# Attention followed by an expert layer: moving one batch's last-column scores to another PSUM pair, and its product forward, in the steady down matmul

## The chip, the cores and the metric

One core of one Trainium2 chip. The metric is the device time of one execution in microseconds (us); a profile of one execution gives the trace that the argument reads. In the views PE is TensorE's matmuls and PEld its weight loads, ACT is ScalarE, DVE VectorE, POOL GpSimd; PSUM is the memory that TensorE writes its results to, in banks, and a pair is two of these. Lines such as L241 are lines of the kernel before; in the changed kernel the lines of the helpers that are named here are the same.

Most executions of a kernel agree within 0.3%. Some have a lower granted TensorE clock (0.981 to 0.989 on average instead of 0.997 to 1.000; one had 0.993) and are about 3 to 5 us longer, whatever the kernel. Where I name times of an experiment below, they are of executions with a clock of 0.997 or more, and I say how many there were.

## The reference, cut to what matters

```python
k_p = k.reshape(B, H, Sp, 8, D).mean(axis=3)        # B=8, H=8, S=576, Sp=72, D=64
v_p = v.reshape(B, H, Sp, 8, D).mean(axis=3)
attn = softmax(scale * q @ k_p^T)                   # per batch and head, 576 x 72
x = (attn @ v_p)  -> [4608 tokens, 512]
h = x @ w_in                                        # 512 -> 2048
out = (h * cos(h)) @ w_out                          # 2048 -> 512
```

A tile of the expert layer has 512 tokens, a batch has 576. So there are nine tiles for eight batches, and tile t + 1 needs the last 64 columns of batch t ("REST" in the kernel) as well as the first columns of batch t + 1.

## The kernel before

Each tile t has an up stage (64 matmuls of 512 columns, cosine on ACT, multiply on DVE) and a down stage (64 matmuls of 512 columns). The attention of the next batch is filled in between the down matmuls. A fill entry `(n, f)` runs `f` just ahead of the n-th down matmul; n is called its *place* here.

Attention is cut in units. Four big ones (256 columns x 4 heads) belong to batch b = t + 1, and REST (64 columns x 8 heads) to batch t. Each unit needs two things:

- *scores*: eight or four matmuls into a pair of PSUM banks, then one exponential on ACT that reads the pair;
- a *product* with the values: matmuls into a pair, then ln, ln, exp on ACT (the inverse of the sums), then two multiplies on DVE that read the pair and write `xT`.

```python
def scores(b, u, pair):
    scores_mm(b, u, pair)          # TensorE, L211
    scores_exp(b, u, pair)         # ACT: ex, L218

def values(b, u, pair, later=None):                 # the "product"
    ...                                             # matmuls, L241
    lnc, inv = inverse_tile(w)                      # lnc: one buffer
    for hp in range(2):
        nc.scalar.activation(out=lnc[half[1 - hp]], in_=pair[half[1 - hp], hp, 0:w], func=ACTF.Ln)   # L247
    nc.scalar.activation(out=inv, in_=lnc, func=ACTF.Exp, scale=-1.0)                                # L248
    def mul():
        for hp in range(2):
            nc.vector.tensor_mul(out=x_out(b, u, half[hp]), ...)                                     # L252
    ...
```

There are three pairs (`banks[0..2]`), which the up stage uses too, and two single banks for the down matmuls. The steady down stage (t = 1 to 6) before:

```python
fill = [(1, lambda: scores(t, REST, banks[1 if 0 < t and b < B else 2])), (12, lambda: values(t, REST, banks[1]))]
...  # (cut: t == 0)
elif b < B:
    fill = [(4, two_(0, 2, 0)), (14, V_(0, 1)), (19, V_(1, 2)),      # first two units: scores, products
            (31, two_(2, 0, 1)), (37, V_(2, 2)), (41, V_(3, 0)),     # last two units
            (42, fill[0][1]), (54, fill[1][1])]                      # REST: scores, product
...
for n, (ms, fc) in enumerate(mms):
    while fi < len(fill) and fill[fi][0] <= n:
        fill[fi][1]()
        fi += 1
    down_mm(obanks[ms % 2], ms, fc)
    if fc == FFCH - 1:
        down_out(t, ms, obanks[ms % 2])     # DVE copy L316, then the output DMA
```

`two_(n, p, q)` makes the scores of units n and n + 1 in pairs p and q; `V_(n, p)` is the product of unit n in pair p.

The softmax here doesn't subtract the row's maximum and nothing guards it: scores larger than these inputs give would overflow.

## Time and profile before

| | before |
|---|---|
| time, median (range, runs) | 305.17 us (304.85 to 305.43, 4) |
| span in the profile | 303.0 us |
| TensorE busy | 292.3 us, 96% |
| one steady down stage, from ACT's table load to the first up matmul | 16.48 us, six times the same |
| TensorE standing still in each | 0.31 us |

With TensorE at 96%, the question is where it still stands, not how busy the others are on average. The prediction below shows the lines and reads them. (It was made with the first three runs, whose median is 305.36.)

### The profile page before, as it was taken

Reading aid. Unit: us, or ns where it says so; the run is one execution under the profiler, and the core shown is the slowest. Engines: PE = TensorE matmul, PEld = TensorE weight load, DVE = VectorE, ACT = ScalarE, POOL = GpSimd, SP = SyncE. Lnnn points to the kernel's source line nnn. Section 1 sums busy time; section 2 is a strip of 40 time slices with the busy share of each in tenths; the row PEclk is TensorE's granted clock in tenths of the full one; section 3 lists DMA queues with packets and bytes.
Section 4 is the critical chain, followed back from the end, with each engine's and each line's share of the span. In section 5 each row is a group of like instructions: output and inputs, shape, how many; then the busy total and the mean of one; then the engine's idle time right before and its main releaser. Section 6 shows DMA issues by size and latency. Waiting matters only on the chain.

```text
span 303.0 us, 4567 instructions
## 1 busy us (share of the span) xinstructions
PE 292.3 (96%) x1766; PEld 141.8 (47%) x1798; DVE 172.8 (57%) x211; ACT 206.8 (68%) x255; POOL 129.8 (43%) x92
## 2 busy tenths in 40 slices
PE   6899999999999999999999999999999999999995
PEld 2545544444544444444444544454444544444444
DVE  6458646564656465736575566656574657425712
ACT  3887896469866986698668876788569856605500
POOL 8553008975963893369534972399000000000000
PEclk9999999999999999999999999999999999999999
DMA  7999999739476935693369426952800330031032
GB/s 144 203 207 206 208 204 195 161 55 172 94 167 88 151 70 129 101 163 82 80 117 165 96 65 126 162 107 54 151 0 2 70 69 0 22 84 35 0 71 71
DMA packets 44006, 32.92 MB, mean 109 GB/s; under 512 B 22096, under 2 KB 39248, under 8 KB 43984
## 3 DMA queue, kind: packets, MB, share of 16 engines
q0 software_dynamic: 19744, 18.07, 38.4%
q1 hardware_dynamic: 24080, 14.42, 20.8%
q8 instruction: 14, 0.23, 0.3%
q10 hardware_dynamic: 160, 0.13, 0.2%
q14 instruction: 8, 0.07, 0.1%
HBM read 36.70 MB, written 9.44 MB: 152 GB/s over the span
## 4 chain that ended last, share of the span: by engine, by line
PE 88%; ACT 5%; issue 2%; DMA 2%; DVE 1%; DVEq 0%; ACTq 0%; POOLq 0%
PE bank L297 41%; PE obank L310 35%; PE bank L241 5%; PE bank L211 3%; DMA q_b<-in_q_dram 2%; ACT lnc L247 2%; ACT ex L218 1%; PE bank L328 1%; DVE xT L252 1%; ACT inv L248 1%; PE obank L157 0%; ACT L285 0%; PE obank L192 0%; ACT cos L304 0%; PE bank L165 0%
## 5 line engine op out<-in xcount | busy, mean ns | idle before, releaser
L310 PE MATMUL obank<-w_out_sb,g_sb 128*128 128x512 bf16 x542 | 130.5, 380 | 0.9
L297 PE MATMUL bank<-xT,w_in_sb 128*128 128x512 bf16 x563 | 125.7, 379 | 1.3
L304 ACT ACTIVATE cos<-bank,half_pi 128x1024 f32<-128x1024 f32 x72 | 80.0, 1113 | 62.2 <-PE bank L297 62.2
L307 DVE TENSOR_TENSOR g_sb<-bank,cos 128x1024 bf16<-128x1024 f32 x72 | 88.1, 1225 | 51.7 <-ACT cos L304 51.7
L297 PEld LDWEIGHTS <-w_in_sb 128*128 128x128 bf16 x576 | 56.1, 98 | 69.0 <-issue 2.8
L310 PEld LDWEIGHTS <-g_sb 128*128 128x128 bf16 x560 | 52.3, 98 | 57.0 <-issue 3.1
L252 DVE TENSOR_TENSOR xT<-bank,inv 64x512 bf16<-64x512 f32 (+1 forms) x72 | 45.3, 629 | 46.7 <-ACT inv L248 45.2
L141 POOL TENSOR_TENSOR kv_st<-kv_st 72x2048 f32<-72x2048 bf16 x12 | 48.7, 4062 | 35.0 <-DMA kv_st<-in_k_dram 35.0
L247 ACT ACTIVATE lnc<-bank 64x512 f32<-64x512 f32 (+1 forms) x72 | 39.2, 544 | 6.6 <-PE bank L241 5.6
L218 ACT ACTIVATE ex<-bank 72x1024 bf16<-72x1024 f32 (+1 forms) x40 | 35.5, 926 | 3.3 <-PE bank L211 3.2
L316 DVE COPY o_sb<-obank 128x512 f32<-128x512 f32 x35 | 24.2, 692 | 17.0 <-PE obank L310 13.4
L142 POOL TENSOR_TENSOR kv_st<-kv_st 72x1024 f32<-72x1024 f32 x12 | 28.2, 2348 | 1.0
L248 ACT ACTIVATE inv<-lnc 128x512 f32<-128x512 f32 (+1 forms) x36 | 21.0, 583 | 1.1
L241 PE MATMUL bank<-ex,vz 72*128 72x256 bf16 (+1 forms) x176 | 20.0, 243 | 0.2 <-ACT ex L218 0.2
L241 PEld LDWEIGHTS <-vz 72*128 72x128 bf16 x176 | 13.6, 97 | 10.2 <-DVE xT L252 1.7
L145 POOL TENSOR_TENSOR kp<-kv_st 72x512 bf16<-72x512 f32 x12 | 15.0, 1268 | 0.5
L211 PE MATMUL bank<-qT,kk 64*72 64x256 bf16 (+1 forms) x192 | 13.6, 252 | 0.9 <-ACT qT L193 0.5
L211 PEld LDWEIGHTS <-kk 64*72 64x72 bf16 x192 | 7.5, 109 | 11.1 <-issue 9.8
L285 ACT ACT_TABLE_LOAD x9 | 11.5, 1283 | 0.9 <-PEq L514 0.7
L288 ACT ACT_TABLE_LOAD x9 | 11.5, 1283 | 0.2
L494 POOL COPY gate<-kk 1x1 bf16<-1x1 bf16 x5 | 0.9, 179 | 24.1 <-DMA kk<-kp 24.1
L84 POOL DMA_DIRECT2D q_b<-in_q_dram x10 | 7.7, 772 | 2.8 <-DMA w_in_sb<-in_moe_w_in_dram 1.4
(55 smaller groups left out, 88.2 us busy)
## 6 DMA issues: line engine op xcount, KB each, us to landing
out_dram<-o_sb SPq DMA_DIRECT2D x70, 128.0 KB, 2.3
kv_st<-in_v_dram POOLq DMA_DIRECT2D x8, 576.0 KB, 13.3
kv_st<-in_k_dram POOLq DMA_DIRECT2D x7, 576.0 KB, 7.9
q_b<-in_q_dram POOLq DMA_DIRECT2D x6, 576.0 KB, 10.2
w_in_sb<-in_moe_w_in_dram POOLq DMA_DIRECT2D x4, 512.0 KB, 13.3
w_out_sb<-in_moe_w_out_dram POOLq DMA_DIRECT2D x4, 512.0 KB, 18.4
q_b<-in_q_dram POOLq DMA_DIRECT2D x4, 288.0 KB, 11.9
g_sb<-in_k_dram SPq DMA_DIRECT2D x1, 576.0 KB, 3.6
```

The costliest lines, as they stand in the source:

```text
L141: add(out=s, in0=x[:, :, 0:4, :], in1=x[:, :, 4:8, :], op=ADD)
L142: add(out=s[:, :, 0:2, :], in0=s[:, :, 0:2, :], in1=s[:, :, 2:4, :], op=ADD)
L211: nc.tensor.matmul(pair[:Sp, bank, c:c + n].rearrange("p (g n) -> p g n", n=64), lhsT=kk[b % 2][half[r], h0 + i, 0:Sp], rhs=att["qT", b][h ...
L218: nc.scalar.activation(out=ex[:, 0:nh * n].rearrange("p (a n) -> p a n", a=2), in_=pair[:Sp, :, 0:nh * n // 2], func=ACTF.Exp, scale=scale ...
L241: nc.tensor.matmul(pair[:, hp, (i // 2) * n:(i // 2 + 1) * n], lhsT=vz[b % 2][:, pj, 2 * hp:2 * hp + 2, :].rearrange("p a d -> p (a d)"), ...
L247: nc.scalar.activation(out=lnc[half[1 - hp]], in_=pair[half[1 - hp], hp, 0:w], func=ACTF.Ln)
L252: nc.vector.tensor_mul(out=x_out(b, u, half[hp]), in0=cols(pair[half[hp], hp, :], u), in1=cols(inv[half[1 - hp]], u))
L297: nc.tensor.matmul(h[:, j, :], lhsT=w_in_sb[fc // 4][:, ki, (fc % 4) * 128:(fc % 4 + 1) * 128], rhs=xT[:, ki, t * TILE:(t + 1) * TILE], st ...
L304: nc.scalar.activation(out=cos, in_=h, func=ACTF.Sin, bias=half_pi[:, :1])
L307: nc.vector.tensor_mul(out=g_sb[:, 2 * fp:2 * fp + 2, :], in0=h, in1=cos)
L310: nc.tensor.matmul(o, lhsT=g_sb[:, fc, ms * 128:(ms + 1) * 128], rhs=w_out_sb[fc // 4][:, fc % 4, :], start=(fc == 0), stop=(fc == FFCH - 1))
L316: nc.vector.tensor_copy(out=o[:, 0:n], in_=ps)
```

## The change

The intent is to let REST's exponential run early, so that its product can stand further from the end of the stage, and the next up stage need not wait for it. The pair that the second product has left (pair 2) takes REST's scores; the third and fourth products move to pairs 0 and 1.

```diff
-            fill = [(1, lambda: scores(t, REST, banks[1 if 0 < t and b < B else 2])), (12, lambda: values(t, REST, banks[1]))]
+            late = 0 < t and b < B
+            fill = [(1, lambda: scores(t, REST, banks[2])), (12, lambda: values(t, REST, banks[2 if late else 1]))]
...
-            fill = [(4, two_(0, 2, 0)), (14, V_(0, 1)), (19, V_(1, 2)), (31, two_(2, 0, 1)), (37, V_(2, 2)),
-                    (41, V_(3, 0)), (42, fill[0][1]), (54, fill[1][1])]
+            fill = [(4, two_(0, 2, 0)), (14, V_(0, 1)), (19, V_(1, 2)), (32, two_(2, 0, 1)), (36, fill[0][1]),
+                    (38, V_(2, 0)), (41, V_(3, 1)), (45, fill[1][1])]
```

## The prediction

> **What bounds the kernel now.** I read the page first: the busy row and the chain of work that ended last.
>
> ```profile
> PE 292.3 (96%) x1766; PEld 141.8 (47%) x1798; DVE 172.8 (57%) x211; ACT 206.8 (68%) x255; POOL 129.8 (43%) x92
> ...
> PE 88%; ACT 5%; issue 2%; DMA 2%; DVE 1%; DVEq 0%; ACTq 0%; POOLq 0%
> ```
>
> TensorE sets the time: 96% busy and 88% of the chain. A change that neither adds nor removes matmuls can therefore only win back the moments in which TensorE stands still. The 5% of ACT and 1% of DVE in the chain say where to look for those, and also cap what there is to win. The changed code is the steady down stage (t = 1 to 6), so next I cut the trace by that stage, from the load of the exponential's table to the first matmul of the next up stage.
>
> ```profile
> 68.25:84.73 16.48, 16.28 (x104) 8.07 (x101) 9.67 (x15) 14.96 (x22) 13.31 (x6) 1.00 0.69 121
> 99.88:116.36 16.48, 16.28 (x105) 8.06 (x102) 9.68 (x15) 14.97 (x22) 16.16 (x7) 1.00 0.49 88
> ...
> 226.37:242.85 16.48, 16.28 (x104) 8.05 (x101) 9.67 (x15) 14.97 (x22) 0.00 (x0) 1.00 0.14 33
> ```
>
> Columns: stretch, its length, busy time of PE, PEld, DVE, ACT, POOL, granted clock, DMA share, GB/s. All six stages last 16.48 us to the hundredth, at full clock, whatever the DMA and GpSimd do, so one stage can be worked out and multiplied by six. I take t = 2. Its part of the chain of waits, in order of time:
>
> ```profile
> 112.79 1.03 PE obank L310 x4
> 113.82 0.30 PE bank L241 x8
> ...
> 114.20 0.38 ACT lnc L247
> 114.59 0.39 ACT lnc L247
> 115.00 0.43 ACT inv L248
> ...
> 115.88 0.44 DVE xT L252
> 116.36 5.99 PE bank L297 x27
> ```
>
> The last product of the stage (the eight 64-column matmuls of the batch before, REST) goes through logarithm, exponential and multiply before the next up matmul may start at 116.36. Now the timeline of the same stretch (start, length, engine, line, operation):
>
> ```profile
> 107.16 1.39 DVE L252 TENSOR_TENSOR xT<-bank,inv 64x512 bf16<-64x512 f32 x2
> ...
> 108.60 0.46 PEld L241 LDWEIGHTS <-vz 72*128 72x128 bf16 x4 [0.19 <-DVE xT L252]
> ...
> 109.43 1.19 ACT L247 ACTIVATE lnc<-bank 64x512 f32<-64x512 f32 x2 [0.17 <-PE bank L241]
> ...
> 111.32 1.19 ACT L247 ACTIVATE lnc<-bank 64x512 f32<-64x512 f32 x2
> ...
> 113.08 0.57 ACT L218 ACTIVATE ex<-bank 72x512 bf16<-72x512 f32 x1
> 113.21 1.39 DVE L252 TENSOR_TENSOR xT<-bank,inv 64x512 bf16<-64x512 f32 x2 [0.50 <-ACT inv L248]
> ...
> 113.94 2.32 PE L310 MATMUL obank<-w_out_sb,g_sb 128*128 128x512 bf16 x10
> 114.20 0.77 ACT L247 ACTIVATE lnc<-bank 64x256 f32<-64x256 f32 x2 [0.54 <-PE bank L241]
> ...
> 116.36 6.85 PE L297 MATMUL bank<-xT,w_in_sb 128*128 128x512 bf16 x30
> ```
>
> The ten down matmuls from 113.94 take 2.32 us with the last one's 0.38, so they start every (2.32 - 0.38)/9 = 0.216 us. The last starts at 115.88; the next could start at 116.10 and starts at 116.36: TensorE stands still for 0.26. It stands still once more, for about 0.05, where REST's product waits for its exponential (113.08 + 0.57 = 113.65; first product matmul at 113.71, 0.27 after its predecessor in the single records instead of 0.22). So there is 0.31 us to win per stage, 6 x 0.31 = 1.9 us in all, 0.6% of 305.36. That is the ceiling.
>
> **What the Trainium skill says.** "TensorE: Matmul & The Clock Gate", section "Wait — 56ns, not 53.3ns?", gives N/2.4 GHz plus about 2.5 ns between starts of warm matmuls, 215.7 ns at 512 columns; this trace has 0.216, so TensorE has no slack besides the two stops. "ScalarE: Activation LUTs", section "What ACT_TABLE_LOAD costs", gives 186 ns plus 0.833 ns per element for an activation with immediate scale, and an overlap of 93 ns back to back. The trace has 1.02 for 1024 columns (formula 1.04), 0.59 for 512 (0.61), 0.38 for 256 (0.40). Two score exponentials start 0.92 apart, with the overlap, but the ln, ln, exp group of one product does not overlap like that: its next group starts 1.89 later (109.43 to 111.32), as each step reads what the last one wrote and there is one lnc buffer. "Perfetto Trace Analysis", section "Matmuls", advises to rotate independent groups through different PSUM banks, so that emptying one overlaps the next group's matmuls. The weight load at 108.60 shows what the present layout lacks: the third product reuses pair 2 and is released by the multiplies of the second (107.16 + 1.39 = 108.55); its matmul still starts on the beat, at 108.74.
>
> **The change part by part.** Counts and shapes stay the same on every engine; the instruction order of both programs confirms it (PE has 3598 rows in each). Four things move.
>
> 1. Second score group from place 31 to 32: one down matmul goes ahead, +0.216. Scores start at 107.10 instead of 106.88, the first exponential at 107.55 instead of 107.33. The pairs are free; no stop.
> 2. REST's scores from place 42 to 36, into pair 2. After the score group (0.56) and four down matmuls, and the 0.31 that separates a down matmul from scores after it in this trace, they are due at 107.10 + 0.56 + 0.65 + 0.01 + 0.31 = 108.63. Pair 2 must have been left by the second product's multiplies: end 108.55, release some 0.05 later, 108.60. It fits with 0.03 to spare. These matmuls move, they are not added: 0.25 earlier in the stage and 0.25 less later.
> 3. Third product at 38 in pair 0, fourth at 41 in pair 1. The third is due at 108.63 + 0.25 + 0.23 + 0.22 = 109.33, against 108.74: 0.59 later (0.25 REST's scores, two places, a little rounding). REST's exponential now lies between the scores' exponentials and this product's logarithm: 107.55 + 2 x 0.92 = 109.39 to 109.96, before the logarithm can start (109.43 + 0.59 = 110.02). So it costs ACT nothing.
> 4. REST's product at 45 instead of 54: nine matmuls, 1.9 us, earlier on TensorE. But this doesn't reach the end whole, since ACT isn't ready for it. ACT: third product from 110.02, fourth from 111.91, REST from 113.80 (1.89 each), its last exponential ends 1.22 later (114.20 to 115.42 before), at 115.02. Before: 115.42. DVE: the fourth product's multiplies start when its inverse ends, 113.21 + 0.59 = 113.80, and last 1.39, to 115.20; REST's two follow (DVE copies the third output block after them now, no longer between) and last 0.87: 116.07. Before: 115.44 + 0.87 = 116.31.
>
> The next up matmul follows 0.05 after the last multiply, at about 116.12, against 116.36: 0.24 us per stage. TensorE would be there at 116.36 - 0.31 = 116.05, so a stop of some 0.07 remains. One item more: in the changed order the wait for these multiplies sits on the weight load ahead of the first up matmul, not on the matmul, so the load can't be done early. A load held in the same way at the start of the kernel (copy of qT ends 8.50, load 8.55, matmul 8.56) lost only 0.01 between load and matmul, so I charge 0.02: 0.22 us. Sum: 6 x 0.22 = 1.3 us; 305.36 - 1.3 = 304.0 (the span of the profile 303.0 to 301.7).
>
> **The rivals.** First, the stop vanishes wholly: nine places earlier looks like 1.9 us of slack against a stop of 0.26, and the time falls by the ceiling, to 303.5. What speaks against it is the ACT row: once the third product is late, ACT and then DVE work through to the end without a pause. Second, the wait for pair 2 takes the place of the one removed. Only 0.03 spare it; every hundredth by which REST's scores slip delays the third product and the whole ACT and DVE chain behind it. A slip of 0.1 leaves 0.12 a stage, 304.6. For it: the release is from exactly those multiplies; against it: the held load at 108.60 cost nothing before. Third, the held weight load costs its full 0.10 at the up stage: 0.14 a stage, 304.5. Fourth, the later output copies or the DMA matter: the copy of block two moves from 114.63 to about 116.1, but its accumulator is wanted only at the next down stage, some 14 us on, and the first multiply of the up stage comes at 119.43. No effect.
>
> **Range and chances.** Mechanisms give 0.12 to 0.31 a stage, 0.7 to 1.9 us; the mean is near 1.3. The runs of before spread over 0.46, so a median carries some 0.2. Time 304.0, range 303.3 to 304.8. Two per cent is 6.1 us, three times the ceiling: faster 0.01, same 0.98, slower 0.01 (an unforeseen stop of over 1 us in each stage).
>
> **What would show it.** In the timeline of t = 2: REST's scores on the beat after four down matmuls, the third product's logarithm about 0.6 later than before, REST's logarithm directly after the fourth product's inverse with no idle time, and DVE's four last multiplies back to back. The stage should last 16.48 - 0.22 = 16.26. If it lasts 16.17, the stop vanished, and my ACT and DVE chain is too long; if over 16.35, the wait for pair 2 or the weight load binds. The prediction is wrong if stages t = 1 to 6 no longer agree with each other or if time moves outside them.

## The result, and the profile after

| | before | changed |
|---|---|---|
| time, median (range, runs) | 305.17 (304.85 to 305.43, 4) | 303.81 (303.58 to 303.91, 4) |
| ratio of the fast runs (95% interval) | | 0.9955 (0.9938 to 0.9972) |
| steady down stage | 16.48 | 16.26 |
| from the table load of t = 1 to that of t = 7 | 189.74 | 188.47 |

A ratio is the mean time of one kernel's fast runs over that of the other's fast runs of the same rounds, so it isn't quite the ratio of the medians. The gain is 1.36 us, 0.45%: clear of noise, and inside two per cent, as forecast. The table loads of t = 1 and t = 7 enclose the six steady ends of stage; between them 1.27 us went, six times 0.21.

The stretches of the changed kernel, in the same columns as in the prediction:

```profile
...
100.06:116.31 16.25, 16.25 (x106) 7.96 (x101) 8.98 (x14) 15.15 (x22) 14.84 (x6) 1.00 0.57 102
...
```

The stage has lost 0.22 us, and all six agree (16.25 or 16.26). DVE has one instruction less in it (14 instead of 15): the copy of the third output block, 0.69 us, has gone behind REST's multiplies, and starts only 0.03 before the first up matmul. Both traces record 1798 weight loads, 211 DVE and 255 ACT instructions in all: only the order has changed. Now the timeline of t = 2 after the change (start, length, engine, line, operation, what ended the idle time):

```profile
107.33 1.39 DVE L252 TENSOR_TENSOR xT<-bank,inv 64x512 bf16<-64x512 f32 x2
...
107.72 2.41 ACT L218 ACTIVATE ex<-bank 72x1024 bf16<-72x1024 f32 x3 [0.68 <-PE bank L211]
...
108.80 0.21 PEld L211 LDWEIGHTS <-kk 64*72 64x72 bf16 x8 [0.42 <-DVE xT L252]
...
110.20 1.20 ACT L247 ACTIVATE lnc<-bank 64x512 f32<-64x512 f32 x2
...
112.13 4.27 PE L310 MATMUL obank<-w_out_sb,g_sb 128*128 128x512 bf16 x19
...
113.98 0.77 ACT L247 ACTIVATE lnc<-bank 64x256 f32<-64x256 f32 x2
113.98 2.28 DVE L252 TENSOR_TENSOR xT<-bank,inv 64x512 bf16<-64x512 f32 x4 [0.50 <-ACT inv L248]
...
114.77 0.42 ACT L248 ACTIVATE inv<-lnc 128x256 f32<-128x256 f32 x1
...
116.28 1.29 DVE L316 COPY o_sb<-obank 128x512 f32<-128x512 f32 x2
116.31 0.76 PEld L297 LDWEIGHTS <-w_in_sb 128*128 128x128 bf16 x5 [0.41 <-DVE xT L252]
116.31 1.04 PE L297 MATMUL bank<-xT,w_in_sb 128*128 128x512 bf16 x4
```

Read it from the end. The first up matmul at 116.31 follows the last of DVE's four multiplies, which end at 113.98 + 2.28 = 116.26. The nineteen down matmuls from 112.13 start (4.27 - 0.38)/18 = 0.216 apart, the last at 116.02; the next could start at 116.24 and starts at 116.31. So a stop of 0.08 us is left of 0.26. The other stop, 0.05 ahead of REST's product, is gone: in the single records that product starts at 111.89, 0.21 after the down matmul ahead of it. DVE's four multiplies stand as one group, since the copy is no longer between them; they start when the fourth product's inverse is ready. REST's logarithm at 113.98 has no idle time before it, where it had 0.54 before: ACT now goes through all three products without a pause from 110.20 on. REST's inverse ends at 114.77 + 0.42 = 115.19, while DVE is busy with the fourth product's two multiplies until 115.37; so at the end DVE binds, and ACT has 0.18 to spare. The three exponentials from 107.72 include REST's.

Here a view misleads. The chain of waits of the same stage:

```profile
112.29 4.10 PE obank L310 x19
116.39 6.78 PE bank L297 x31
```

ACT and DVE have vanished from it, as though TensorE ran through. They haven't: the wait now sits on the weight load, not on the matmul, and the modelled length of a matmul (0.38 for a beat of 0.216) covers a stop of 0.08. The starts of the matmuls show the stop; the chain does not. Nor is the view of waits a measure of it:

```profile
PEld L297 <- DVE xT L252: 2.5, 6, 0.4
```

That is 2.5 us of weight loads held in six stages, while TensorE itself lost 6 x 0.08 = 0.5 us.

### The profile page after: what moved, and what is told of

It reads as the page before. It is cut to its first block, busy times and chain, and to the rows that moved or that the text cites. A ratio compares the mean times of both kernels' runs of the same rounds, so it can differ in the third digit from the quotient of the medians.

```text
span 302.1 us, 4605 instructions
## 1 busy us (share of the span) xinstructions
PE 294.0 (97%) x1798; PEld 141.6 (47%) x1798; DVE 172.3 (57%) x211; ACT 206.8 (68%) x255; POOL 129.8 (43%) x92
## 4 chain that ended last, share of the span: by engine, by line
PE 85%; DMA 10%; POOL 2%; ACT 1%; issue 0%; DVE 0%; POOLq 0%; ACTq 0%
PE obank L310 39%; PE bank L297 37%; DMA w_out_sb<-in_moe_w_out_dram 6%; PE bank L241 5%; DMA w_in_sb<-in_moe_w_in_dram 4%; PE bank L211 3%; PE bank L328 1%; POOL kv_st L84 1%; POOL kp L384 1%; POOL q_b L84 1%; ACT L285 0%; ACT cos L304 0%; ACT ex L218 0%; POOL identity masks.py:197 0%; DVE o_sb L316 0%
## 5 line engine op out<-in xcount | busy, mean ns | idle before, releaser
L310 PE MATMUL obank<-w_out_sb,g_sb 128*128 128x512 bf16 x560 | 132.5, 380 | 0.5 <-DMA w_out_sb<-in_moe_w_out_dram 0.5
```

Of the source, the lines that this page charges most:

```text
L310: nc.tensor.matmul(o, lhsT=g_sb[:, fc, ms * 128:(ms + 1) * 128], rhs=w_out_sb[fc // 4][:, fc % 4, :], start=(fc == 0), stop=(fc == FFCH - 1))
```

## The experiments

The theory is that of the prediction: in the steady stage, ACT works without a pause through the third and the fourth product (ln, ln, exp, twice), and DVE then through the four multiplies of the fourth and REST's product, so the *third product's place* sets when the next up stage may start, until TensorE's own work sets it. REST's product has slack, provided that its exponential comes early and that its multiplies stand ahead of DVE's third copy. The chief rival is the simple reading of the change: REST's product is nine places earlier, and each place is worth something. All runs below were correct. The stage length is that of t = 2, and the other five agree with it within 0.01 us. The runs lay on several chips (the first four below the changed kernel on one, the last four on another), on which the kernel before took 304.90 and 305.20 at a clock of 0.997 or more; so the comparison rests on the stages, and the times are its check.

| run | places: group, REST's scores, third, fourth, REST's product | stage, expected | stage, measured | time (executions at clock 0.997 or more) |
|---|---|---|---|---|
| changed | 32, 36, 38, 41, 45 | 16.26 | 16.26 | 303.81 (4) |
| product_47 | 32, 36, 38, 41, **47** | 16.26 | 16.26 | 304.03 (4) |
| product_48 | 32, 36, 38, 41, **48** | 16.95 | 16.98 | 308.08 (3) |
| group_31 | **31**, 36, 38, 41, 45 | 16.26 | 16.26 | 303.94 and 303.98 (2) |
| rest_scores_35 | 32, **35**, 38, 41, 45 | 16.45 | 16.46 | 304.92 (3) |
| third_40 | 32, 36, **40**, **43**, 47 | 16.69 | 16.69 | 306.32 and 306.78 (2) |
| third_37 | **31**, 36, **37**, **40**, 45 | 16.17 | 16.18 | 303.05 (5) |
| scores_only | 32, 36, 38, 41, **54** | 16.95 | 16.98 | 308.01 and 308.32 (2) |
| product_only_47 | before, with REST's product at **47** | 17.7 | 17.74 | 312.51 (3) |

### product_47 and product_48: how much slack has REST's product?

```diff
-                    (38, V_(2, 0)), (41, V_(3, 1)), (45, fill[1][1])]
+                    (38, V_(2, 0)), (41, V_(3, 1)), (47, fill[1][1])]     # product_48: 48
```

> The changed kernel with REST's product at place 47 instead of 45, still ahead of the copy of the third output block. Chain theory (ACT and DVE from the third product on set the end; REST's product has slack): the steady stage stays at 16.26 us, time as the changed kernel, 303.8. Place theory (each place that REST's product is earlier wins time): 0.43 us per stage lost, 16.69, until the whole gain is gone, 305.2 or more.

> One place further, 48, so that DVE's copy of the third output block is issued ahead of REST's multiplies. Chain theory with DVE's order: DVE is busy with the fourth product until about 15.3 us into the stage, the copy takes 0.7, so REST's multiplies end at about 16.9 and the stage lasts 16.95 (0.69 more than changed, 0.47 more than before): 6 x 0.69 = 4.1 us, 307.9. If the order on DVE does not matter and only ACT's chain does: 16.26, 303.8.

Two places later changed nothing: 16.26. One more place cost 0.72 us per stage, 4 us in the whole. The place differs by a single beat of 0.216 between the two, and TensorE's work not at all. What differs is that the third output block ends at place 47, so that from 48 on its copy is issued to DVE ahead of REST's multiplies. DVE in product_48, end of t = 2:

```profile
119.18 1.39 DVE L252 TENSOR_TENSOR xT<-bank,inv 64x512 bf16<-64x512 f32 x2 [0.50 <-ACT inv L248]
...
120.60 0.69 DVE L316 COPY o_sb<-obank 128x512 f32<-128x512 f32 x1
...
121.32 0.86 DVE L252 TENSOR_TENSOR xT<-bank,inv 64x256 bf16<-64x256 f32 x2
```

REST's inverse was ready at 120.39, so its multiplies could have started when the fourth product's ended, at 120.57; the copy holds them up until 121.32. The place theory falls with the first run, and the importance of DVE's order is shown by the pair. (The profile of product_48 fell in an execution with a low clock early on. Its steady stages ran at full clock, and the run scores_only below, at full clock throughout, shows the same 16.98.)

### group_31: is the shift of the second score group worth anything?

```diff
-(32, two_(2, 0, 1)), (36, fill[0][1]),
+(31, two_(2, 0, 1)), (36, fill[0][1]),
```

> The changed kernel with the second score group back at place 31. Chain theory: the third product keeps its place 38, and it alone starts the chain, so the shift by one is worth nothing: stage 16.26, 303.8. If the shift was part of the gain (scores later, fewer stops elsewhere): over 16.26, up to 16.48.

The stage stayed at 16.26 in all six. This part of the change is idle. Two of four executions, the profiled one among them, had a clock of 0.989 and 0.983 and took 307.0 and 307.2; in the profiled one the low clock lies in the first tenth of the span, ahead of the steady stages. Therefore the median of all four (305.50) is not used.

### rest_scores_35: the wait for pair 2

```diff
-(32, two_(2, 0, 1)), (36, fill[0][1]),
+(32, two_(2, 0, 1)), (35, fill[0][1]),
```

> REST's scores one place earlier, at 35. My step 2: the second product's multiplies leave pair 2 about 8.66 us into the stage, release at 8.72, and at place 36 the scores are due at 8.75; at 35 they are due at 8.53 and must wait 0.19. The chain behind slips by that: stage 16.45, six times 0.19 = 1.15 us, 304.9. If pair 2 is free much earlier than I worked out: 16.26, 303.8.

The timeline of t = 2 in this run:

```profile
107.40 1.39 DVE L252 TENSOR_TENSOR xT<-bank,inv 64x512 bf16<-64x512 f32 x2
...
108.84 0.21 PEld L211 LDWEIGHTS <-kk 64*72 64x72 bf16 x8 [0.63 <-DVE xT L252]
```

The second product's multiplies end at 107.40 + 1.39 = 108.79, and REST's scores start at 108.84, 0.05 later, although they were one place earlier. The stage grew by 0.20. So the wait for pair 2 is real, and the change just clears it, though one place earlier would not: REST's scores at 36 start 8.75 us into the stage, where the pair is free from about 8.72.

### third_40 and third_37: where does the chain start?

```diff
# third_40
-                    (38, V_(2, 0)), (41, V_(3, 1)), (45, fill[1][1])]
+                    (40, V_(2, 0)), (43, V_(3, 1)), (47, fill[1][1])]
# third_37
-(32, two_(2, 0, 1)), (36, fill[0][1]), (38, V_(2, 0)), (41, V_(3, 1)), (45, fill[1][1])]
+(31, two_(2, 0, 1)), (36, fill[0][1]), (37, V_(2, 0)), (40, V_(3, 1)), (45, fill[1][1])]
```

> Third product at 40 instead of 38, fourth at 43, REST's product at 47 (shown or not shown to be free by the run with 47 alone). Chain theory: the ACT and DVE work behind the third product starts 2 x 0.216 = 0.43 us later and so does the next up stage: 16.69, 6 x 0.43 = 2.6 us, 306.4. Rival (the chain starts elsewhere, for instance at the fourth product or at REST's exponential): no change, 16.26.

> Second score group at 31, third product at 37, fourth at 40, the rest as changed. Chain theory: the chain starts 0.216 us earlier than in the changed kernel, which is more than the 0.08 us of stop that the changed kernel still has; the stop goes, TensorE alone sets the stage: 16.17, 6 x 0.08 = 0.5 us less, 303.3. Rival (the remaining stop is the cost of a weight load that is held and can't be done early): 16.26 stays, 303.8.

Two places later gave 16.69, two beats of 0.216 more; since place 47 for REST's product cost nothing above, the delay comes from the third and fourth products. One place earlier gave 16.18. This is the run group_31 with these two products one place forward, so the 0.08 belongs to them. The end of t = 2 in third_37:

```profile
111.79 4.27 PE L310 MATMUL obank<-w_out_sb,g_sb 128*128 128x512 bf16 x19
...
113.42 2.28 DVE L252 TENSOR_TENSOR xT<-bank,inv 64x512 bf16<-64x512 f32 x4 [0.50 <-ACT inv L248]
...
115.89 1.46 PE L297 MATMUL bank<-xT,w_in_sb 128*128 128x512 bf16 x6
```

The multiplies end at 115.70. The last down matmul starts at 111.79 + 18 x 0.216 = 115.68, and the up matmul at 115.89, on the beat. The stop is gone. The first up matmul's weight load still waits for the multiplies here, but is released at 115.75, 0.14 ahead of its matmul, and so this run alone doesn't show what a load costs that is held to the last moment. The changed kernel does: there load and matmul start within 0.01 of each other, and the second up matmul follows 0.226 after the first (116.310 to 116.536 in the single records), where it is 0.216 here and 0.215 in the kernel before. In all eight traces in which load and matmul start together it is 0.225 to 0.227, in the other four 0.215 or 0.216. So a load held to the last moment costs 0.01, not 0.08, and the rival, that it was the rest of the stop, falls.

Which of the two products starts the chain was not tried apart, but the traces tell. In the changed kernel the fourth product's matmuls end by 111.19 as recorded and its logarithm starts at 112.09, straight after the third product's exponential; the fourth was there some 0.8 us before ACT was. The third product's matmuls end at 110.10, and its logarithm follows at 110.20. In group_31 ACT even stands idle for 0.27 until the third product comes, with the same stage. So it is the third.

This version is faster than the kernel before, by a ratio of 0.9931 (0.9918 to 0.9944): 303.05 (302.95 to 303.24, five runs). It never ran in the same rounds as the changed kernel; that it is faster than that one too is shown by the stages, 16.18 against 16.26.

### scores_only and product_only_47: each part of the change alone

```diff
# scores_only: from the changed kernel
-(45, fill[1][1])]
+(54, fill[1][1])]
# product_only_47: from the kernel before
-(41, V_(3, 0)), (42, fill[0][1]), (54, fill[1][1])]
+(41, V_(3, 0)), (42, fill[0][1]), (47, fill[1][1])]
```

> One part alone: REST's scores at 36 in pair 2 and the products moved as in the change, but REST's product left at place 54. Chain theory: ACT starts REST's logarithm at 14.3 us into the stage as before, but DVE is busy with the fourth product until 15.3 and then with the copy until 16.0; REST's multiplies end at 16.9, stage 16.95, slower than both kernels: 307.9. Place theory: the product has its old place, so the time is that of before, 305.2.

> The other part alone: the kernel before with only REST's product moved from 54 to 47, scores left at 42 in pair 1. REST's exponential still stands behind the fourth product on ACT and ends 13.8 us into the stage, so TensorE, due at 12.3, waits until 13.83 and has 17 down matmuls left: stage 17.7, 1.24 more than before, 6 x 1.24 = 7.4 us, 312.6. Rival (the place of the product is the gain, the scores' place doesn't matter): 16.2 to 16.3, about 304.

In scores_only the end of t = 2 looks as in product_48: DVE's multiplies of the fourth product from 114.77 to 116.16, the copy from 116.19 to 116.88, REST's multiplies from 116.92 to 117.78, and the first up matmul at 117.83. The copy stands between the fourth product's multiplies and REST's, and the up matmul waits for it all. The scores' move without that of REST's product is a loss of 0.50 us per stage against the kernel before. (It brings the later third product and the new pairs with it.) The product's move alone is a larger one:

```profile
114.84 0.57 ACT L218 ACTIVATE ex<-bank 72x512 bf16<-72x512 f32 x1
115.47 0.39 PE L241 MATMUL bank<-ex,vz 72*128 72x64 bf16 x8 [1.40 <-ACT ex L218]
```

REST's exponential is still behind the fourth product on ACT and ends at 115.41; TensorE waits for it and the stage lasts 17.74. So neither part gains anything alone, at the places tried; the gain needs both.

### A last stop outside the change, and the changed kernel again

```diff
# third_37_last_14: third_37, and
-(12, lambda: values(t, REST, banks[2 if late else 1]))
+(14, lambda: values(t, REST, banks[2 if late else 1]))
```

> The version with the third product at 37, and in the last down stage with a product (t = 7, not steady, not part of the change) REST's product at place 14 instead of 12: in the changed kernel TensorE stands there for 0.32 us, waiting for REST's exponential; two down matmuls (0.43) cover it. Expected 0.3 us less than with the third product at 37 alone, near 302.8, and the steady stages stay at 16.18. If another wait sets the end of that stage: as the version before it, 303.1.

> The changed kernel once more, on the same chip as the best version, so that the two are compared in the same rounds: 303.8, stages of 16.26.

The changed kernel gave 303.72 (six executions), its stages 16.25 to 16.26. The new version gave 303.14 (five executions at full clock, 302.76 to 303.83; a sixth took 307.69). In the traces, the part from the table load of t = 7 to the end went from 44.96 in third_37 to 44.65, 0.31 less, as expected. In the times this isn't seen: 303.14 on this chip against 303.05 for third_37 on another. In its profiled execution the table load of t = 1 came at 68.77, in third_37's at 68.39, and this start of the kernel, which no edit here touches, varied by that much. So the 0.31 is shown by the trace alone.

## Why the prediction was right

It was right in its mechanism as well as in its number: each step of its sum can be set beside the trace. Where two small errors cancelled, this is said.

- *The ceiling of 0.31 us per stage.* third_37 reached 16.18, 0.30 below the kernel before, with TensorE on its beat at the end.
- *The second score group one place later.* Predicted as no stop and no gain; group_31 shows it idle.
- *REST's scores at 36 clear the wait for pair 2 by 0.03.* They start 8.75 us into the stage, as worked out, and one place earlier the wait appeared, 0.20 long for 0.19 expected.
- *The third product 0.59 later.* Its logarithm starts 10.14 us into the stage instead of 9.56: 0.58. The prediction's sum of times was right, but not the split given in brackets (0.25 for REST's scores and two places make 0.68): the product moved by one place, 0.22, and REST's scores hold up the down matmuls by 0.36, with the changes into and out of them (109.28 for a start due at 108.92).
- *ACT's and DVE's chain up to 16.19 us into the stage (116.07 in the times of the kernel before).* The last multiply ends at 16.20. The four multiplies together take 2.28 instead of the 2.26 that two groups of 1.39 and 0.87 add up to. The reason given for the 1.89 of a product on ACT, that each step reads what the last one wrote, isn't shown: the second logarithm reads nothing of the first, and yet starts 0.60 after it, at a length of 0.59. The 1.89 itself came from the trace. (The page's 186 ns are for an immediate scale and an immediate bias; the quotation leaves out the bias, and the durations fit.)
- *The charge of 0.02 for the held weight load.* The wait did move to the load, as predicted, but the term was oversized, and in the wrong place: the matmul started 0.05 after the last multiply both before (116.31 to 116.36) and after (116.26 to 116.31). The load's cost is the 0.01 ahead of the second up matmul, outside the stage as cut here. That the multiplies took 0.02 longer and the sum stayed 0.22 is luck, on a scale of 0.02.
- *Six times 0.22, 1.3 us, 304.0.* Measured: 0.22 per stage, 1.36 in the medians, 303.81. From one table load to the next it is 0.21, as the held load takes 0.01 back.

The first rival, that the stop vanishes wholly, was wrong for this kernel, and for the stated reason: the third product had been moved back. third_37, which moves it forward again, is what that rival described. The second rival was excluded by rest_scores_35 (the change stands just on the right side of that wait), the third by the 0.01 that the held load costs in the changed kernel. Of the fourth, that the later output copies matter, nothing is seen: from one table load to the next the changed kernel keeps what its stage gained, to within 0.02.

The 3598 rows of TensorE that the prediction counts in both programs stand in no view; that nothing was added is shown by the equal counts of the two traces, above.

One forecast missed: the profile's span, 302.1 instead of 301.7. In that execution the table load of t = 1 came at 68.64 instead of 68.25 before, 0.39 later, so time did move outside the steady stages, which the prediction had named as a sign against it. The code ahead of that point isn't changed, and in other profiles at full clock, of kernels with the same start, it came between 68.39 and 68.77, and at 68.75 in product_only_47, which is the kernel before up to that point; I count it as variation of the start, whose cause was not looked for.

## What to carry to other kernels

When the main engine is nearly full, measure the starts of its instructions at the end of a repeated stage, and follow the side engines back from there to the place where they last had idle time: the work after that idle moment is what must come earlier; here, moving REST's product among places behind it (45 or 47) changed nothing. Check also what a new place does to the order on an in-order engine: one place here put a copy of 0.69 us ahead of the multiplies that the next stage waits for, and turned a gain of 0.22 into a loss of 0.50. Here the product and the scores that it rests on had to be moved together, since either alone made the kernel slower.

## What the Trainium skill lacked or had wrong

- "TensorE: Matmul & The Clock Gate", section "Back-to-back issue gap", says that a stream of weight loads and matmuls of 512 columns sustains about 131 ns per matmul. Here such a stream, with a load for each matmul, starts one every 216 ns, as that page's other figure has it (N/2.4 GHz plus about 2.5 ns).
- The same page, section "The mechanism", says that weight loads overlap with matmuls in flight only where the row group differs, beside a sentence that also allows the background buffer. In this trace the overlap is the rule for the same rows: the 128-row load for the first up matmul of t = 3 in the kernel before starts at 115.88, together with the last 128-row down matmul.
- I found no page with a figure for the change between matmuls of 128 rows and scores of 64 rows (it belongs to "TensorEngine Tiling (Array Packing)", section "Key Properties"). In the trace of before the first scores start 0.31 us after the down matmul ahead of them instead of 0.22, and the first down matmul 0.20 after the last scores, which otherwise follow each other, two at a time, at 0.11: an estimate of 0.19 us for each group of scores.
- "Perfetto Trace Analysis", section "Tensor Engine Instruction (MATMUL, LD_WEIGHTS)", warns that the ends of matmuls are estimates, but not that the stop before a matmul can hide in them: 0.08 us of waiting was absent from the chain of waits here, since a matmul is drawn 0.38 long on a beat of 0.216.
- I found no page that says how long the release from DVE to TensorE takes: 0.05 us from the recorded end of the multiply to the recorded start of the matmul or load, in every trace here in which the first up matmul or its load waited for one.
